# A second output layer as Strassen products in two sweeps, in a fused attention and two-layer gated network kernel

## The chip, the cores and the metric

The kernel runs on one core of one Trainium2 chip. The metric is the device time of one execution in microseconds. Before the change the median of three runs is 1741.35 us (1739.97 to 1743.14).

## What is computed

```
kv  = k^T v                      per batch (8) and head (8), 576 tokens, width 64
a   = q kv ;  a = a / rms(a) * g
x   = a as 4608 tokens x 512
x   = (sigmoid(x w_gate) * (x w_val)) w_out          512 -> 1536 -> 512
out = elu(x w_in) w_out2                             512 -> 2048 -> 512
```

All arrays are float32, and the weights arrive as 64-bit words that the kernel decodes.

## The kernel before, in words

**Tokens and groups.** The 4608 tokens are 12 blocks of 384. Two blocks make a group (`NG` = 6), and a hidden pair `fp` is two hidden chunks of 128. The kernel runs the first layer for all six groups (attention of group g+1 is mixed into the products of group g), then the second layer for all six. The second layer takes two stages a group: `in2` (eight pairs) and `out2`.

**Three matmuls for one.** Every float32 operand is split into a high and a low fp32r part. `matmul3` (L346 to L350) issues high x high, high x low, low x high into one accumulator, so each product of the text is three matmuls on lines L348, L349, L350.

**Strassen in the input layers.** `quad` computes a 2x2 block product (two hidden chunks by two token blocks) with seven products of six matmuls of 384 columns. `sides` (L450 to L466) prepares the token sides: differences on POOL and DVE (L458 to L463), then for each of seven sides a high part on ACT (L464) and a low part on DVE (L465). The sums over products are DVE additions that read PSUM (L485). Weight sums are made by `sums` on POOL when a weight is decoded, and come back with the stored high and low parts through `stream`.

**The plain output layer.** `out2` (L602 to L620) takes each hidden chunk and each token block, lets `split` (L546 to L552) make a J tile (high on ACT L550, low on DVE L552), and multiplies it by the chunk's 512 weights:

```python
for f in range(NF2):
    if f % 2 == 0:
        s, ld = stream("O", f // 2)
    for blk in in_blocks(f, NF2):
        j, dj = split(*hs[f // 2][f % 2, blk])
        for i in range(TPB):
            matmul3(acc[blk][i].slot, j.slot[:, 0, i*P:i*P+P], j.slot[:, 1, i*P:i*P+P],
                    v[:, f % 2, 0, :], v[:, f % 2, 1, :], f == 0, f == NF2 - 1)
```

A stage is 16 chunks x 2 blocks x 3 token chunks x 3 = 288 matmuls of 512 columns with the token chunk stationary, into six PSUM banks. Copies (L557, L558) and stores (L620) follow the last chunk.

**What sets the order.** `Plan` holds tasks with planned durations, buffer classes and due times, and writes out one fixed order for each engine and for SP, which issues every DMA. PE's order is the order in which the program adds products. Buffers that matter here: `S` (weights, 5 of 8 KB per partition), `J` (3 of 3 KB), `v` (54 blocks of 1.5 KB), `raw` (3), `wk` (4), `kv` (3), and eight PSUM banks in classes `psi` and `psa`. The first group runs plain products (`in1_plain`) while weights are decoded (`decode`, L260 to L303).

Of the kernel before, what the change touches and what calls it, by code (L numbers as in the profile page):

```python
# [9 lines left out]
F32 = mybir.dt.float32  # L10
# [11 lines left out]
P = 128  # L22
# [13 lines left out]
MMW = DM / 2400 + 0.0126  # L36
# [15 lines left out]
class Task:  # L52
    def __init__(self, eng, dur, fn, after, bufs, due, seq):
        self.eng, self.dur, self.fn, self.bufs, self.slack, self.seq = eng, dur, fn, bufs, due, seq
        self.after = {id(t): t for t in after if t is not None}.values()
        self.next, self.wait, self.ready, self.early, self.started = [], 0, 0.0, None, None


class Plan:
# [12 lines left out]
    def add(self, eng, dur, fn, after=(), bufs=(), due=None, queue=None):  # L72
# [6 lines left out]
        return t  # L79

# [36 lines left out]
    def round(self):  # L117
        self.set_due()
        for t in self.tasks:
            t.wait, t.ready = len(t.after), 0.0  # L120
            for b in t.bufs:
                b.left, b.slot = 0, None
# [28 lines left out]
        def begin(t, at):  # L151
# [7 lines left out]
            push(at + t.dur, "end", t)  # L159

# [45 lines left out]
def tile_kernel(ctx: ExitStack, tc: tile.TileContext, kv, kvtail, qt, g2, w1, w2, out):  # L206
# [49 lines left out]
    last_hi = [None]  # L256

    def decode(layer, fp, after=None):

        src, idx = (w1, "gvo".index(layer)) if layer in "gvo" else (w2, "IO".index(layer))  # L260
        order = (2 * fp, 2 * fp + 1) if layer in "oO" else (2 * fp + 1, 2 * fp)
        wh, wp = plan.buf("wk", "wh"), plan.buf("wk", "wp")
        word = []
        for n, f in enumerate(order):
# [14 lines left out]
        sa = plan.buf("S", "dec" if layer in "gvo" else "dec2")  # L279
        if layer in "oO":  # L280
            hi = lambda: sa.slot.rearrange("q b t n -> q (b t n)").rearrange("q (f t n) -> q f t n", f=2, t=2)
            x_hi, x_lo, src_w = (lambda: hi()[:, :, 0, :]), (lambda: hi()[:, :, 1, :]), lambda: wh.slot
        else:
            x_hi, x_lo = (lambda: sa.slot[:, :, 0, :]), (lambda: sa.slot[:, :, 1, :])
            src_w = lambda: wh.slot.rearrange("q f (k n) -> q (f k) n", k=2)
        h = add("ACT", 1.05, lambda: nc.scalar.activation(x_hi(), src_w(), AF.Copy), [w, last_hi[0]], [wh, sa])
        last_hi[0] = h
        l = add("DVE", 1.3, lambda: nc.vector.tensor_tensor(x_lo(), src_w(), x_hi().bitcast(F32), op=ALU.subtract), [h], [wh, sa])
        if layer in "oO":
            d = (wo1 if layer == "o" else wo2)[fp]  # L290
            written[layer, fp] = [dma(P * 8192, lambda: nc.sync.dma_start(
# [443 lines left out]
```

## Time and profile before

| | |
|---|---|
| median of 3 runs | 1741.35 us |
| the profiled execution | 1741.11 us, its span 1739.3 us, mean granted clock 0.991 |
| PE busy | 1704.1 us, 98% of the span, 9359 matmuls |
| DVE, ACT, POOL busy | 971.6, 757.1, 258.6 us |
| DMA | 431.57 MB, 68.4% of 16 engines' span on SP's queue |

The rest of the execution's time, 1.8 us, lies around the span. A busy PE means that matmul records cover the time; since matmuls are pipelined and their ends modelled, the pace is read from starts and counts, not from the duration of one.

### The profile page before, as it was taken

To read this page: it belongs to the slowest core of one execution; us is meant where nothing else is said; L and a number is where in the kernel's file an instruction comes from. 1 tells how busy PE (TensorE), PEld (TensorE's weight loads), DVE (VectorE), ACT (ScalarE), POOL (GpSimd) and SP (SyncE) were. 2 spreads that over 40 slices of the span, in tenths; PEclk is the share of its full clock that TensorE was granted. 3 is DMA by queue.
4 is the path that set the end of the run, shared out by engine and by line. 5 is a ranking of instruction groups with operands and counts; after the bars stand their busy time and mean duration, and the time that the engine had idled before them with its cause. 6 is when DMAs were issued, how large, how long until landed. Compare 5 with 4: busy or idle time off the path is not lost.

```text
span 1739.3 us, 25106 instructions
## 1 busy us (share of the span) xinstructions
PE 1704.1 (98%) x9359; PEld 1609.7 (93%) x9359; DVE 971.6 (56%) x1752; ACT 757.1 (44%) x1527; POOL 258.6 (15%) x244
## 2 busy tenths in 40 slices
PE   6899999999999999999899999999999999999998
PEld 5799999999999999999899998898998998998987
DVE  5466647854485376458444465465465455555542
ACT  4455433542263245226213364364353453443542
POOL 0001236411140132124122001001001001001000
PEclk8899999999999999999999999999999999999999
DMA  9597988798579768867867476475574673773751
GB/s 347 177 347 262 339 276 291 258 352 320 220 267 358 258 242 318 324 231 259 312 252 283 146 257 220 166 266 184 197 281 142 224 271 129 248 266 116 260 203 59
DMA packets 94443, 431.57 MB, mean 248 GB/s; under 512 B 10608, under 2 KB 29040, under 8 KB 66928
## 3 DMA queue, kind: packets, MB, share of 16 engines
q1 hardware_dynamic: 94320, 429.96, 68.4%
q8 instruction: 74, 1.21, 0.3%
q14 instruction: 49, 0.40, 0.1%
HBM read 353.37 MB, written 76.55 MB: 247 GB/s over the span
## 4 chain that ended last, share of the span: by engine, by line
PE 91%; DVE 4%; DMA 3%; ACT 1%; issue 1%; SPq 0%; DVEq 0%; ACTq 0%
PE psi L348 23%; PE psi L350 23%; PE psi L349 22%; PE psa L349 6%; PE psa L350 6%; PE psa L348 6%; PE psa L396 2%; PE psa L370 2%; DMA wsI<-S 2%; PE psa L435 1%; PE psa L372 1%; DVE J L552 1%; DMA kv<-kv 1%; DVE wk L272 1%; DMA S<-wsv 0%
## 5 line engine op out<-in xcount | busy, mean ns | idle before, releaser
L485 DVE TENSOR_TENSOR v<-v,psi 128x384 f32<-128x384 f32 x540 | 298.4, 553 | 336.2 <-PE psi L350 328.1
L348 PE MATMUL psi<-x,S 128*128 128x384 f32 x1056 | 361.8, 343 | 1.1 <-DMA S<-wsv 1.1
L349 PE MATMUL psi<-x,S 128*128 128x384 f32 x1056 | 355.0, 336 | 0.0
L350 PE MATMUL psi<-x,S 128*128 128x384 f32 x1056 | 354.9, 336 | 0.0
L552 DVE TENSOR_TENSOR J<-v,J 128x384 fp32r<-128x384 f32 x336 | 200.3, 600 | 257.1 <-ACT J L550 257.1
L550 ACT ACTIVATE J<-v 128x384 fp32r<-128x384 f32 x336 | 175.3, 523 | 326.2 <-PE psa L349 116.6
L348 PE MATMUL psi<-xt,S 128*128 128x384 f32 x648 | 220.6, 340 | 2.7 <-DMA S<-wsv 2.7
L350 PE MATMUL psi<-xt,S 128*128 128x384 f32 x648 | 217.3, 335 | 0.0
L349 PE MATMUL psi<-xt,S 128*128 128x384 f32 x648 | 217.0, 335 | 0.0
L348 PEld LDWEIGHTS psi<-x,S 128*128 128x128 f32 x1056 | 199.9, 189 | 4.5 <-DMA S<-wsv 1.4
L349 PEld LDWEIGHTS psi<-x,S 128*128 128x128 f32 x1056 | 199.8, 189 | 0.4 <-DVE x L443 0.2
L350 PEld LDWEIGHTS psi<-x,S 128*128 128x128 f32 x1056 | 199.5, 189 | 0.0
L521 POOL TENSOR_TENSOR v<-v,v 128x384 f32<-128x384 f32 x90 | 98.5, 1098 | 410.8 <-DVE v L485 366.1
L460 POOL TENSOR_TENSOR v<-v,v 128x384 f32<-128x384 f32 x22 | 24.9, 1130 | 773.8 <-DVE v L458 747.5
L348 PEld LDWEIGHTS psi<-xt,S 128*128 128x128 f32 x648 | 122.0, 188 | 3.8 <-issue 3.0
L596 ACT ACTIVATE v<-v 128x384 f32<-128x384 f32 x144 | 75.4, 524 | 108.8 <-DVE v L485 108.8
L349 PEld LDWEIGHTS psi<-xt,S 128*128 128x128 f32 x648 | 121.9, 188 | 0.0
L350 PEld LDWEIGHTS psi<-xt,S 128*128 128x128 f32 x648 | 121.9, 188 | 0.0
L489 ACT ACTIVATE v<-psi 128x384 f32<-128x384 f32 x108 | 53.1, 492 | 137.1 <-PE psi L350 130.9
L350 PE MATMUL psa<-S,J 128*128 128x512 f32 x288 | 112.7, 391 | 0.0
L350 PE MATMUL psi<-S,J 128*128 128x512 f32 x288 | 112.6, 391 | 0.0
L349 PE MATMUL psa<-S,J 128*128 128x512 f32 x288 | 112.2, 389 | 0.0
(96 smaller groups left out, 2979.8 us busy)
## 6 DMA issues: line engine op xcount, KB each, us to landing
S<-wsI SPq DMA_DIRECT2D x48, 1024.0 KB, 5.1
S<-wsO SPq DMA_DIRECT2D x48, 1024.0 KB, 5.0
S<-wso SPq DMA_DIRECT2D x36, 1024.0 KB, 6.2
S<-wsI SPq DMA_DIRECT2D x48, 768.0 KB, 5.9
raw<-w SPq DMA_DIRECT2D x68, 512.0 KB, 6.4
S<-wsg SPq DMA_DIRECT2D x24, 1024.0 KB, 5.8
S<-wsv SPq DMA_DIRECT2D x24, 1024.0 KB, 5.2
S<-wsg SPq DMA_DIRECT2D x30, 768.0 KB, 6.8
```

Of the source, the lines that this page charges most:

```text
L348: nc.tensor.matmul(acc, wh, xh, start=first, stop=False, skip_group_check=more)
L349: nc.tensor.matmul(acc, wh, xl, start=False, stop=False, skip_group_check=more)
L350: nc.tensor.matmul(acc, wl, xh, start=False, stop=last, skip_group_check=more)
L370: nc.tensor.matmul(o, k[:, 0, c, :], k[:, 1, c, :], start=(c == 0), stop=False)
L396: nc.tensor.matmul(v[lo - t0:hi - t0, i, :], qb.slot[:, lo - j * BLK:hi - j * BLK], kvb[b % 2][:, p, :], start=True, stop=True)
L460: k2 = add("POOL", T_POOL, lambda t=t2, a=b22, b=t1: nc.gpsimd.tensor_tensor(t.slot, a.slot, b.slot, op=ALU.subtract), [k1, d22], [t2, b22 ...
L485: return add("DVE", T_DVE, lambda: nc.vector.tensor_tensor(dst.slot, a.slot, bank[k].slot[:, :BLK], op=ALU.add), after, [dst, a, bank[k]])
L489: s1 = add("ACT", T_ACT, lambda: nc.scalar.activation(t1.slot, bank["a"].slot[:, :BLK], AF.Copy), [p1], [t1, bank["a"]])
L521: t = add("POOL", T_POOL, lambda r=r, b=b: nc.gpsimd.tensor_tensor(r.slot, r.slot, b.slot, op=ALU.mult), [d, s], [r, b])
L550: hi = add("ACT", T_ACT, lambda: nc.scalar.activation(j.slot[:, 0, :], f.slot, AF.Copy), [d], [j, f])
L552: lo = add("DVE", 0.5, lambda: nc.vector.tensor_tensor(j.slot[:, 1, :], f.slot, j.slot[:, 0, :].bitcast(F32), op=ALU.subtract), [hi], [j, f])
L596: a1 = add("ACT", T_ACT, lambda e=e, b=b: nc.scalar.activation(e.slot, ps_or_v(b), AF.Relu, scale=-1.0), [d], [e, b])
```

## The change

It touches five things.

1. **Second output layer** (`out_stage`, `Tokens`, `out2`). Each stage becomes seven products for each of eight hidden pairs, 9 matmuls of 256 columns each (3 token chunks x 3), token chunk stationary, half of the outputs moving. Four accumulators a, b, c, d take two PSUM banks each, all eight. In sweep 1, pair by pair, a and c then b and d are summed; `middle` copies a and adds up outputs from b, c and d; in sweep 2 a, c and d take three further products for each pair; `end` forms three outputs.
2. **Token sides of the output layer.** The sides are made in place on POOL in the hidden buffers: one subtraction in `in2` (L586), three in `out_stage` (L650, L651, L656) for each pair. `split` now takes two blocks at a time (128x768).
3. **Two-block buffers.** Features and hidden values sit in `hp` (21 of [P, 2, 384]); `sides` works on 128x768; `v` shrinks to 11, `J` becomes 4 of 6 KB.
4. **Weights in 4 KB pieces.** `S` becomes 7 of 4 KB. A pair of an input layer is loaded as four DMAs (512, 512, 512, 256 KB) where it was two; a pair of the second output layer as 512, 512, 512 and 256 KB where it was one of 1024 KB.
5. **Decode in place.** High and low parts are written over the raw words; the decodes of second-layer weights move from four after each of groups 1 to 4 to six, six and four after groups 1 to 3. The units of the first group run in another order, and the first key/value loads use the three `kv` buffers alone.

The core of the diff:

```diff
-    slots("v", 54, [P, BLK], F32)
-    slots("S", 5, [P, 4, 2, 256], F32R)
-    slots("J", 3, [P, 2, BLK], F32R)
+    slots("hp", 21, [P, 2, BLK], F32)
+    slots("v", 11, [P, BLK], F32)
+    slots("S", 7, [P, 2, 2, 256], F32R)
+    slots("J", 4, [P, 2, 2, BLK], F32R)
...
+    def stream(layer, fp):
+        d, res = (ws2 if layer == "I" else ws1["gv".index(layer)])[fp], {}
+        for names, view in ((("A11", "S2"), d[:, 0:5:4]), (("S1", "S3"), d[:, 3:6:2]), (("A12", "S4"), d[:, 1:7:5]), (("A22",), d[:, 2:3])):
+            t, ld = load(view, written[layer, fp])
+            res.update({n: (t, i, ld) for i, n in enumerate(names)})
+        return res
...
-            t, view, ld = load_kv(b, p, "wk" if first and p > 1 else "kv")
+            t, view, ld = load_kv(b, p, "kv")
...
+    def t1_in_place(hp, t):
+        k = add("POOL", T_POOL, lambda: nc.gpsimd.tensor_tensor(
+            hp[0].slot[:, 1, :], hp[0].slot[:, 1, :], hp[0].slot[:, 0, :], op=ALU.subtract), [t["11"], t["12"]], [hp[0]])
+        return hp, [t["11"], k], [t["21"], t["22"]]
...
+    def out_stage(layer, hs, parts, mm_of, finish):
+        nf = len(hs)
+        acc = {k: [plan.buf("psa" if k in "ac" else "psi") for _ in parts] for k in "abcd"}
...
+        def first_half(fp):
+            hp, d1, _ = hs[fp]
+            s, ld = stream_out(layer, fp, 0, 0)
+            j, jv, dj = split(lambda: hp[0].slot, 2, d1, hp[0], "JA")
+            last["a"] = product("a", 0, j, jv, 0, s, ld + dj, fp == 0)
+            last["c"] = product("c", 1, j, jv, 1, s, ld + dj, fp == 0)
+            return dj
+        def second_half(fp, dj):
+            hp, d1, d2 = hs[fp]
+            s, ld = stream_out(layer, fp, 0, 1)
+            H = lambda k, e: hp[k].slot[:, e, :]
+            k2 = add("POOL", T_POOL, lambda: nc.gpsimd.tensor_tensor(H(0, 1), H(1, 1), H(0, 1), op=ALU.subtract), dj + d2, hp)
+            k3 = add("POOL", T_POOL, lambda: nc.gpsimd.tensor_tensor(H(0, 0), H(0, 1), H(0, 0), op=ALU.subtract), [k2], [hp[0]])
+            j, jv, dj2 = split(lambda: hp[0].slot, 2, [k3], hp[0], "JB")
+            last["b"] = product("b", 0, j, jv, 1, s, ld + dj2, fp == 0)
+            last["d"] = product("d", 1, j, jv, 0, s, ld + dj2, fp == 0)
+            return add("POOL", T_POOL, lambda: nc.gpsimd.tensor_tensor(H(0, 1), H(1, 0), H(0, 1), op=ALU.subtract), dj2 + d2, hp)
+        k4, dj = {}, {}
+        for fp in range(nf + 1):
+            if fp < nf:
+                dj[fp] = first_half(fp)
+            if fp:
+                k4[fp - 1] = second_half(fp - 1, dj[fp - 1])
+        got = finish.middle(acc, last)
+        done = {}
+        for fp in range(nf):
+            hp, _, d2 = hs[fp]
+            s, ld = stream_out(layer, fp, 1, 0)
+            j, jv, dj_ = split(lambda hp=hp: hp[1].slot, 2, d2 + [k4[fp]], hp[1], "JA")
+            done["a"] = product("a", 1, j, jv, 0, s, ld + dj_, False, got["a"])
+            s4, ld4 = stream_out(layer, fp, 1, 1)
+            done["c"] = product("c", 0, j, jv, 1, s4, ld4 + dj_, False, got["c"])
+            j, jv, dj_ = split(lambda hp=hp: hp[0].slot[:, 1:2, :], 1, [k4[fp]], hp[0], "JB")
+            done["d"] = product("d", 0, j, jv, 0, s, ld + dj_, False, got["d"])
+        finish.end(acc, done)
...
+    W2 = (0, 6, 6, 4, 0, 0)
```

PE, at the start of the output stage of the first group of the second layer. `psa` are accumulators, S the weights, J the token chunks. Before:

```order
L348 MATMUL psa_155<-S_134,J_135 128x512
L349 MATMUL psa_155<-S_134,J_135 128x512
L350 MATMUL psa_155<-S_134,J_135 128x512
L348 MATMUL psa_156<-S_134,J_135 128x512
L349 MATMUL psa_156<-S_134,J_135 128x512
```

Now:

```order
L420 MATMUL psa_136<-S_113,J_115 128x256
L421 MATMUL psa_136<-S_113,J_115 128x256
L419 MATMUL psa_137<-S_113,J_115 128x256
L420 MATMUL psa_137<-S_113,J_115 128x256
L421 MATMUL psa_137<-S_113,J_115 128x256
```

A matmul now moves 256 columns; a bank takes two token chunks and the next bank the third. Over the program 1728 matmuls of 512 columns are gone and 3024 of 256 are there; the 6840 of 384 columns stay.

POOL, in sweep 1 of the same stage, from the third pair on (`hp` are hidden buffers, written in place); before, POOL had only the sides of the next group there (L459, L460, L463):

```order
L650 TENSOR_TENSOR hp_90<-hp_93,hp_90 128x384
L651 TENSOR_TENSOR hp_90<-hp_90 128x384
L650 TENSOR_TENSOR hp_91<-hp_84,hp_91 128x384
L651 TENSOR_TENSOR hp_91<-hp_91 128x384
L656 TENSOR_TENSOR hp_90<-hp_93,hp_90 128x384
L650 TENSOR_TENSOR hp_86<-hp_92,hp_86 128x384
L651 TENSOR_TENSOR hp_86<-hp_86 128x384
L656 TENSOR_TENSOR hp_91<-hp_84,hp_91 128x384
```

Three subtractions for each pair are new work on POOL; those of the first two pairs stand ahead of this place, among the last pairs of `in2`. From here to the last pair's L651 there are 16.

DVE, at the end of sweep 1 and the start of sweep 2 (L686 is the low part of a J, L536 that of a side of the next group, L754 an addition out of an accumulator):

```order
L536 TENSOR_TENSOR x_72<-hp_82,x_72 128x2x384
L686 TENSOR_TENSOR J_115<-hp_95,J_115 128x2x384
L686 TENSOR_TENSOR J_118<-hp_88,J_118 128x2x384
L536 TENSOR_TENSOR xt_73<-hp_78,xt_73 128x2x384
L686 TENSOR_TENSOR J_116<-hp_77,J_116 128x2x384
L536 TENSOR_TENSOR x_71<-hp_94,x_71 128x2x384
L754 TENSOR_TENSOR wk_122<-wk_123,psi_134 128x512
L754 TENSOR_TENSOR wk_122<-wk_123,psi_132 128x256
L754 TENSOR_TENSOR wk_123<-wk_122,psa_138 128x512
L754 TENSOR_TENSOR wk_123<-wk_122,psa_139 128x256
L754 TENSOR_TENSOR wk_123<-wk_123,psi_133 128x512
L754 TENSOR_TENSOR wk_123<-wk_123,psi_135 128x256
```

The third row is the last J of sweep 1. From the first J of the third pair to it DVE has 12 J halves and 5 other instructions with two inputs in SBUF. The six additions run without a split between them, and the next row after them is the first J of one block in sweep 2.

## Rows read from the trace of the kernel before

**Rows 1.** The page: busy time of the engines, and the granted TensorE clock in 40 slices (tenths).
```profile
PE 1704.1 (98%) x9359; PEld 1609.7 (93%) x9359; DVE 971.6 (56%) x1752; ACT 757.1 (44%) x1527; POOL 258.6 (15%) x244
...
PEclk8899999999999999999999999999999999999999
```

**Rows 2.** Busy time by stretch: start:end, length, then each engine's busy time with its instructions, the granted clock, the DMA engines' share and GB/s. First key/value products, rest of the first group's plain products, rest of the first layer, second layer.
```profile
0.00:30.00 30.00, 16.36 (x84) 12.75 (x84) 13.60 (x32) 14.37 (x29) 1.63 (x8) 0.84 0.89 334
30.00:174.00 144.00, 134.76 (x775) 128.50 (x774) 90.15 (x156) 77.90 (x145) 5.32 (x4) 0.94 0.75 273
174.00:991.00 817.00, 809.16 (x4759) 795.10 (x4758) 481.61 (x849) 319.14 (x634) 214.96 (x203) 1.00 0.77 280
991.00:1739.00 748.00, 743.87 (x3748) 673.32 (x3746) 386.24 (x718) 345.73 (x721) 36.71 (x30) 1.00 0.58 205
```

**Rows 3.** The same view for one output stage and the input stage after it, and for 60 us inside an output stage.
```profile
1049.60:1115.30 65.70, 65.70 (x290) 53.94 (x289) 30.44 (x52) 24.18 (x49) 7.34 (x6) 1.00 0.48 170
1115.30:1173.60 58.30, 58.30 (x338) 58.28 (x337) 35.74 (x72) 34.13 (x74) 0.00 (x0) 1.00 0.72 260
...
1300.00:1360.00 60.00, 60.00 (x265) 49.24 (x264) 27.73 (x46) 21.21 (x44) 7.34 (x6) 1.00 0.45 163
```

**Rows 4.** PE in order of time at the stages' seams: start, duration (both us), instruction.
```profile
1049.63 0.39 PE L348 MATMUL psa<-S,J 128*128 128x512 f32 x1
...
1115.09 0.39 PE L350 MATMUL psa<-S,J 128*128 128x512 f32 x1
1115.31 0.33 PE L348 MATMUL psi<-x,S 128*128 128x384 f32 x1
...
1173.58 0.39 PE L348 MATMUL psa<-S,J 128*128 128x512 f32 x1
```

**Rows 5.** Groups by line and shape: count, busy us, mean ns of one, idle before. One of the six groups of 512-column matmuls, the float32 matmuls of 128 columns, and three groups of weight loads (PEld).
```profile
L348 PE MATMUL psa<-S,J 128*128 128x512 f32 x288 | 112.1, 389 | 0.0
...
L396 PE MATMUL psa<-kvb,v 128*128 128x128 f32 x256 | 41.9, 292 | 0.0
...
L348 PEld LDWEIGHTS psi<-x,S 128*128 128x128 f32 x1056 | 199.9, 189 | 4.5 <-DMA S<-wsv 1.4 <-DVE v L485 0.9
...
L348 PEld LDWEIGHTS psa<-S,J 128*128 128x128 f32 x288 | 54.1, 188 | 10.9
...
L396 PEld LDWEIGHTS psa<-kvb,v 128*128 128x128 f32 x256 | 37.0, 198 | 3.7 <-issue 3.6
```

**Rows 6.** PE and its weight loads in order of time: six matmuls of 128 columns in a row, merged (start, whole length).
```profile
398.41 0.83 PE L396 MATMUL psa<-kvb,v 128*128 128x128 f32 x6
...
398.24 0.81 PEld L396 LDWEIGHTS psa<-kvb,v 128*128 128x128 f32 x6
```

**Rows 7.** Groups by line and shape on DVE, ACT and POOL.
```profile
L485 DVE TENSOR_TENSOR v<-v,psi 128x384 f32<-128x384 f32 x540 | 298.4, 553 | 336.2 <-PE psi L350 328.1 <-ACT J L550 5.7 <-ACT v L597 1.1
L552 DVE TENSOR_TENSOR J<-v,J 128x384 fp32r<-128x384 f32 x336 | 200.3, 600 | 257.1 <-ACT J L550 257.1
...
L318 DVE TENSOR_TENSOR S<-wk,S 128x1024 fp32r<-128x1024 f32 x20 | 25.9, 1294 | 11.5 <-ACT S L315 11.5
...
L557 DVE COPY kv<-psi 128x512 f32<-128x512 f32 x6 | 4.2, 692 | 15.1 <-PE psi L350 15.1
...
L550 ACT ACTIVATE J<-v 128x384 fp32r<-128x384 f32 x336 | 175.3, 523 | 326.2 <-PE psa L349 116.6 <-PE psi L349 101.7 <-PE psa L350 51.2
...
L521 POOL TENSOR_TENSOR v<-v,v 128x384 f32<-128x384 f32 x90 | 98.5, 1098 | 410.8 <-DVE v L485 366.1
```

**Rows 8.** POOL and DVE in order of time where both work on SBUF (the sides of a group, made beside an output stage).
```profile
1573.68 1.21 POOL L460 TENSOR_TENSOR v<-v,v 128x384 f32<-128x384 f32 x1 [1.02 <-ACT x L464]
1574.86 2.62 POOL L459 TENSOR_TENSOR v<-v,v 128x384 f32<-128x384 f32 x2
...
1576.52 1.37 DVE L552 TENSOR_TENSOR J<-v,J 128x384 fp32r<-128x384 f32 x1
...
1582.27 0.55 DVE L552 TENSOR_TENSOR J<-v,J 128x384 fp32r<-128x384 f32 x1
1582.74 0.55 DVE L465 TENSOR_TENSOR xt<-v,xt 128x384 fp32r<-128x384 f32 x1
1583.21 0.55 DVE L465 TENSOR_TENSOR x<-v,x 128x384 fp32r<-128x384 f32 x1
```

**Rows 9.** POOL's multiplications of L521: shortest, median and longest in ns.
```profile
L521 POOL TENSOR_TENSOR v<-v,v x90: 994/1016/1920, 241.9 to 941.5; 128x384 f32<-128x384 f32 x90
```

**Rows 10.** DMA issues: count, KB each, median us from issue to landing.
```profile
S<-wsO SPq DMA_DIRECT2D x48, 1024.0 KB, 5.0
S<-wso SPq DMA_DIRECT2D x36, 1024.0 KB, 6.2
...
kv<-kv SPq DMA_DIRECT2D x30, 512.0 KB, 7.7
```

**Rows 11.** PE where it waited in the first layer (in brackets the idle time and its releaser).
```profile
48.44 0.80 PE L370 MATMUL psa<-kv 128*128 128x128 f32 x2 [5.14 <-DMA kv<-kv]
...
70.22 0.98 PE L435 MATMUL psa<-ident,v 128*128 128x128 f32 x6 [1.86 <-DVE v L427]
...
855.86 0.44 PE L348 MATMUL psi<-x,S 128*128 128x384 f32 x1 [1.06 <-DMA S<-wsv]
```

More of the change, by code (lines that the diff above doesn't have):

```diff
@@ L79, in add, with follow @@
         return t
+    def follow(self, chain, t):
+        if chain:
+            t.behind = chain[-1]
+            chain[-1].followed.append(t)
+        chain.append(t)
     def set_due(self):
@@ L119, in round @@
         for t in self.tasks:
-            t.wait, t.ready = len(t.after), 0.0
+            t.wait, t.ready = len(t.after) + (t.behind is not None), 0.0
             for b in t.bufs:
@@ L159, in begin @@
             push(at + t.dur, "end", t)
+            for d in t.followed:
+                d.wait -= 1
+                if not d.wait:
+                    push(max(at, d.ready), "ready", d)
         for t in self.tasks:
@@ L286, in decode @@
[L286 to L291, printed above, removed]
-                out=d.rearrange("q f t n -> q (f t n)"), in_=sa.slot.rearrange("q b t n -> q (b t n)").bitcast(F32)), [h, l], [sa])]
-            return sa, [h, l]
@@ new lines, in load @@
+    def load(view, after, early=15.0):
+        t = plan.buf("S")
+        ld = dma(P * 4096, lambda: nc.sync.dma_start(out=t.slot[:, :view.shape[1]].bitcast(F32), in_=view), after, [t], early=early)
+        plan.follow(chain, ld)
+        return t, [ld]
+    def stream(layer, fp):
[3 more added lines that the diff above has]
+            res.update({n: (t, i, ld) for i, n in enumerate(names)})
+        return res
@@ new lines, in fresh @@
+        sums = add_up(wh, ld, sf)
+        t, la = load(d[:, 0:2], written[layer, fp])
+        res["A11"], res["A12"] = (t, 0, la), (t, 1, la)
+        for i in (0, 2):
+            x = plan.buf("S")
+            src = lambda i=i: quarters(sf)[:, i:i + 2, :]
+            h = add("ACT", 0.6, lambda x=x, src=src: nc.scalar.activation(x.slot[:, :, 0, :], src(), AF.Copy), sums, [sf, x])
+            h.early = 12.0
+            plan.follow(chain, h)
+            l = add("DVE", 0.75, lambda x=x, src=src: nc.vector.tensor_tensor(
+                x.slot[:, :, 1, :], src(), x.slot[:, :, 0, :].bitcast(F32), op=ALU.subtract), [h], [sf, x])
+            written[layer, fp] = written[layer, fp] + [dma(P * 4096, lambda x=x, i=i: nc.sync.dma_start(out=d[:, 3 + i:5 + i], in_=x.slot.bitcast(F32)), [h, l], [x])]
+            res[f"S{i + 1}"], res[f"S{i + 2}"] = (x, 0, [h, l]), (x, 1, [h, l])
@@ L467, in sides, with product @@
         return X, done
     def quad(layer, fp, X, done, weights=stream):
-        (sa, sb_), (ld_a, ld_b) = weights(layer, fp)
+        W = weights(layer, fp)
         bank = {k: plan.buf("psi") for k in "abcd"}
-        def product(k, half, i, x, first, last, after=()):
-            s, ld = (sa, ld_a) if half == "A" else (sb_, ld_b)
+        def product(k, name, x, first, last, after=()):
+            s, i, ld = W[name]
             def mm():
@@ L565, in out1, with split @@
+    x2_there = {}
+    def split(view, n, after, b, kind):
+        j = plan.buf("J", kind)
+        jv = lambda t: j.slot[:, :n, t, :]
+        hi = add("ACT", 0.24 + 0.32 * n, lambda: nc.scalar.activation(jv(0), view(), AF.Copy), after, [j, b])
+        hi.early = 14.0
+        lo = add("DVE", 0.25 + 0.4 * n, lambda: nc.vector.tensor_tensor(jv(1), view(), jv(0).bitcast(F32), op=ALU.subtract), [hi], [j, b])
+        return j, jv, [hi, lo]
     def out1(g, hs):
-        acc = {blk: [plan.buf("psi" if blk == 0 else "psa") for _ in range(NCC)] for blk in range(2)}
+        acc = {blk: [plan.buf("psi" if blk else "psa") for _ in range(NCC)] for blk in range(2)}
@@ L623, in tile_kernel, with mm @@
+    def out2(g, hs):
+        def mm(bank, q, ws, xs, first):
+            lo, hi = Tokens.COLS[q]
+            for i in range(lo, hi):
+                o, r = bank.slot[:, (i - lo) * 256:(i - lo) * 256 + 256], slice(i * P, i * P + P)
+                matmul3(o, xs[0][:, r], xs[1][:, r], ws[0], ws[1], first and i == lo, True, not (first and i == lo))
+        out_stage("O", hs, [6 * MMH, 3 * MMH], mm, Tokens(g))
     nc.vector.memset(gcol, 0.0)
```

449 lines of the change are left out of this document (256 added, 193 removed).

## The prediction, on record before the change was timed

> **What bounds the kernel now.** I read the busy times first: PE is covered for 98% of the span at the full granted clock, DVE for 56%, ACT for 44%, POOL for 15% [rows 1]. Then the stretches: the second layer is 748 us with 4 us of PE idle, the first layer after its first group 817 us with 8 us, and only the first 174 us lose more (23 us idle and a clock of 0.84 and 0.94) [rows 2]. So time falls if PE has fewer columns to stream, and only where the next engine keeps up. The stage that the change rewrites is seen in the seams: an output stage runs from 1049.63 to 1115.31, 65.68 us for 288 matmuls, and the input stage behind it to 1173.58, 58.27 us for 336 [rows 4]. PE does not wait in either, while DVE works 30 of 66 us and POOL 7 [rows 3].
>
> **The pace of a matmul of 256 columns.** 384 columns cost 58.27 / 336 = 173.4 ns [rows 4]; 512 cost 60 / 265 = 226.4 ns [rows 3]. That is 0.414 ns a column, so 128 columns fewer than 384 give 173.4 - 53 = 120 ns. The trace has no matmul of 256 columns, so I bound it. From above: not more than the 173.4 ns of 384 columns, which carries the same weight load. From below: six float32 matmuls of 128 columns, each with a load, take 0.83 us [rows 6]; less the 0.29 us that the last one is recorded with [rows 5], they start 0.54 / 5 = 108 ns apart. A load's record is 188 to 198 ns whatever the matmul [rows 5], yet pairs follow at 108 and 173, so the record is latency, and loads do not hold PE at 120. I take 120, on the line through two shapes of the same data type.
>
> **Part 1, the output stage.** 1728 matmuls of 512 columns go, 3024 of 256 come: 504 a stage. 504 x 0.120 = 60.5 us, against 65.7: 5.2 us less, 31 us over six stages. This is the gain; what follows takes from it.
>
> **Part 2, the sides on POOL and DVE in sweep 1.** A pair takes PE four products of nine matmuls, 4.32 us. Beside it POOL makes three subtractions and DVE two low parts of 768 columns. The trace shows that such instructions exclude each other: DVE's low part that starts at 1576.52 takes 1.37 us instead of 0.55 and ends 0.41 us after POOL's second instruction of that run does, at 1577.48 [rows 8]. From the same rows: POOL and one DVE instruction of 384 take 2.62 / 2 = 1.31 us; DVE alone starts one every 0.47 us; so POOL holds the SBUF access for about 0.84 us of its 0.99 [rows 8, 9]. A DVE low part of 768 columns holds it longer by 384 x 1.16 ns (1294 ns for 1024 columns against 0.55 us for 384 [rows 7, 8]): about 0.9 us. A pair alone needs 3 x 0.84 + 2 x 0.9 = 4.3 us of it in 4.32. By the order, from the third pair to the last low part of sweep 1 it is 16 POOL instructions and 17 of DVE, 13.4 + 15.3 = 28.7 us, in the 15 half steps (2.16 us each, 32.4 us) before PE needs that part. The first two pairs' sides are made in the input stage, and two buffers of each J kind give about 4 us of slack. It fits, at 89%, with little left when an instruction comes late: between 0 and 4 us a stage are lost; I take 1.0. It is nearest to the row for the access alone, since no chain there is longer than the slack.
>
> The Trainium skill ("SBUF — State Buffer", "Who interferes with whom") has a rule against this place: a VectorE instruction with two SBUF inputs and a GpSimd one that reads SBUF lock each other out for the whole instruction. The trace agrees on the lock and gives a shorter hold, 0.84 of 0.99 us and 0.47 of 0.55 [rows 8, 9]. Whole instructions would make 16 x 0.99 + 17 x 1.0 = 32.8 us for the 32.4, a sweep without slack, and the sum 10 us or more higher; without a lock it would be 6 us lower. I go by the measured holds.
>
> **Part 3, between the sweeps.** Sweep 2 adds into c and d, so DVE must first have read b, c and d. The order has six additions in a row and then a low part of 384 columns. By rows, 0.69 us for 512 columns and 0.69 - 128 x 1.08 ns x 2 = 0.41 for 256 [rows 7]: 3 x 1.10 + 0.47 = 3.8 us from about 0.2 us before b ends. PE has d of sweep 1 and a and c of sweep 2 in between, 3.24 us. It waits 0.6 us for d (0.3 to 1.0; not a gain). From the end of a stage to the next input stage b's banks are free, and 2 us of products run on them while DVE clears d: no wait.
>
> **Part 4, weights.** A pair of the output layer loads 1.75 MB instead of 1 MB. A stage moves 170 GB/s x 65.7 us = 11.2 MB now [rows 3], 17.5 MB then, 280 GB/s at about 0.8 of the DMA engines. The first layer runs at 280 GB/s and 0.77 for 817 us [rows 2] with few waits such as the 1.06 us at 855.86 [rows 11]. With seven buffers a load in sweep 2 goes out 7.6 us or more ahead of its use; such loads land in 5.0 to 6.2 us [rows 10]. Cost nothing; the cover gone, a load late by 1 us costs that each time. The input stages load the same bytes in four pieces, with 10 us of lead. SP issues 478 DMAs more, each behind the release of a buffer that PE needs no sooner.
>
> **Part 5, the first layer.** The same 384-column matmuls, so no gain by count. The first group can move either way. Against it: the fourth key/value load waits for a buffer; a load lands in 7.7 us [rows 10], some 2 us later than now. For it: the 5.14 us at 48.44 and 1.86 us at 70.22 [rows 11], with the lower clock around them, are up for a new order. Later, six decodes where four ran add some 8 MB to groups 1 and 2, 50 GB/s on 280 [rows 2]: 0.9 of the DMA engines. Unknown: -6 to +12 us, taken as 0. Its price is nearest to the row of the 817 us, which shows that this stretch absorbs transfers.
>
> **The sum.** 504 x 0.120 + 1.0 + 0.6 + 0.2 (the seam that the 65.68 hold) = 62.3 us a stage, 3.4 less. Six stages: 20 us. The profiled execution took 1741.11 us (1739.3 us of span and 1.8 around it), so 1721; it stands 0.2 us below the median of the runs, and I leave the number at **1721 us**.
>
> **Rivals.**
> 1. *No wait shows and the first group gains.* For it: the 28.7 us do fit, and 7 us of waits in the first 71 us are there to be lost [rows 11]. 1741 - 31 - 4 = 1706.
> 2. *The SBUF access becomes the bound of sweep 1 (slower).* Each hand-over between POOL and DVE adds to 4.3 us a pair; if what one pair is late is passed to the next, a sweep stretches. It decides at 4.6 us a stage with Part 3's 0.6, or 0.6 us a pair. With 1.2 us a pair (access taken in turn by 5.8 instructions with 0.2 us between) over eight pairs it is 9.6 us less the 2 us that the early pairs give: 1741 + 6 x (7.6 + 0.6 - 5.2) = 1759. For it: 4.3 of 4.32. Against it: head start and slack, 89% by the order.
> 3. *The first layer pays.* DMA at 0.9 of its time and decodes in place make weights late: +15 us on 1721, 1736, about no change. For it: the wait at 855.86 and the first slices' load. Against it: 0.77 with 8 us of idle in 817.
> 4. *Weight loads set the pace at 256 columns (slower).* Halfway between 120 and 173, 147 ns: 74.1 us a stage, 1741 + 6 x (74.1 + 1.6 - 65.7) = 1801. It decides at 127 ns with the waits of Parts 2 and 3. For it: no row has 256 columns, and the counts of the order leave no doubt that they will be there. Against it: 108 ns at 128 columns, with a load each.
>
> **How the numbers follow.** My case 0.52 (1713 to 1732), rival 1 0.17 (1703 to 1713), rival 2 0.14, rival 3 0.12 (half of it faster, half within 0.2%), rival 4 0.05. Two tenths of a per cent, 3.5 us, is what a measurement of this kernel can tell from no change. Faster: 0.52 + 0.17 + 0.06 = 0.75; the same 0.06; slower 0.14 + 0.05 = 0.19. The range takes the first case with rivals 1 and 3 and the near end of rival 2: 1703 to 1746. My case and rival 1 alone, 1703 to 1732, hold 0.69.
>
> **What would show it.** Right: matmuls of 256 columns 120 ns apart; an output stage of 61 to 63 us; input stages at 58.3; waits of PE below 1 us at the seam of the sweeps, put down to L754 or L686; POOL's L650 and L651 and DVE's L686 with mean times a third above their shortest. Wrong: a pace above 127 ns; PE waiting for L686 or L651 at every pair of sweep 1; PE waiting for loads of `wsO` in sweep 2; the first 991 us of the span moved by more than 8 us.

## The result and the profile after

The changed kernel takes 1765.22 us (median of 4 runs, 1763.76 to 1770.66) where the kernel before takes 1742.24 on the same chip: a ratio of 1.0136, 95% interval 1.0109 to 1.0164. It is slower, by 23 us; the forecast was 1721 and faster. The profiled execution has a span of 1761.9 us.

The page of the changed kernel: busy times, as [rows 1], and PE's busy tenths in 40 slices.

```profile
PE 1691.4 (96%) x10655; PEld 1662.5 (94%) x10655; DVE 1125.7 (64%) x1694; ACT 786.4 (45%) x1432; POOL 538.4 (31%) x435
...
PE   5999999999999999999999998998998998998998
```

PE has 13 us less to do and is covered for 96% instead of 98%: the time went into waits. POOL's time has doubled. The slices with an 8 stand one in three in the second layer: the loss returns once in each group.

The stretches, as [rows 2, 3]: the second layer, the first output stage, the input stage after it, and the last output stage.

```profile
994.70:1757.50 762.80, 731.49 (x5042) 725.44 (x5040) 528.23 (x724) 381.23 (x685) 290.23 (x207) 0.98 0.78 251
1053.60:1123.00 69.40, 62.57 (x505) 62.16 (x504) 50.41 (x49) 29.56 (x43) 35.08 (x22) 0.95 0.72 234
1123.00:1181.90 58.90, 58.88 (x339) 58.25 (x338) 40.24 (x74) 34.56 (x73) 14.87 (x13) 1.00 0.85 277
1696.80:1757.40 60.60, 60.60 (x505) 60.44 (x504) 34.87 (x41) 24.67 (x36) 25.52 (x19) 1.00 0.66 210
```

The two output stages to compare are the second and the fourth row. Both stream the same 504 matmuls of 256 columns. The last one, which has no next group behind it, is 60.6 us of PE without a gap at the full clock; the other is 69.4 us with 6.8 us of PE idle and a clock of 0.95. The loss is in the stage that also makes the sides of the next group: DVE 50 us instead of 35, POOL 35 instead of 26.

PE at the seams, as [rows 4]: first output stage, first matmul after it, last output stage.

```profile
1053.58 0.28 PE L419 MATMUL psa<-S,J 128*128 128x256 f32 x1
...
1122.97 0.28 PE L421 MATMUL psi<-S,J 128*128 128x256 f32 x1
1123.10 0.34 PE L419 MATMUL psi<-x,S 128*128 128x384 f32 x1
...
1696.82 0.28 PE L419 MATMUL psa<-S,J 128*128 128x256 f32 x1
...
1757.16 0.28 PE L421 MATMUL psi<-S,J 128*128 128x256 f32 x1
```

From the first matmul to the last, the five output stages with sides take 69.39, 69.99, 70.34, 69.02 and 69.78 us, and the last 60.34 for 503 steps, 120.0 ns a matmul. The balance against the trace of before:

| stretch | before, us | after, us | difference |
|---|---|---|---|
| up to the second layer's first matmul | 991.39 | 994.75 | +3.4 |
| six input stages, each | 58.07 to 58.09 | 58.63 to 58.65 | +3.3 in all |
| five output stages with sides, each | 65.45 to 65.46 | 69.02 to 70.34 | +21.2 in all |
| last output stage | 65.09 | 60.34 | -4.8 |
| seams between stages | | | -0.5 in all |
| last matmul | 1734.48 | 1757.16 | +22.7 |

What PE waited for in the first output stage (engine, line, releaser: total us, times, longest).

```profile
ACT J L684 <- PE psa L420: 18.5, 12, 3.6
...
PE psa L419 <- DVE wk L754: 5.0, 1, 5.0
...
PE psi L421 <- DVE J L686: 1.9, 1, 1.9
```

PE has two waits: 1.9 us for the last low part (L686) of sweep 1, and 5.0 us for the additions between the sweeps (L754). The first row is ACT's wait for PE before the high parts. What DVE and POOL did ahead of them, in order of time (start, duration, instruction, in brackets idle time and its releaser; the fence has DVE):

```profile
1058.85 1.81 DVE L686 TENSOR_TENSOR J<-hp,J 128x768 fp32r<-128x768 f32 x1 [1.19 <-ACT J L684]
...
1074.59 1.77 DVE L686 TENSOR_TENSOR J<-hp,J 128x768 fp32r<-128x768 f32 x1
1076.28 1.77 DVE L529 TENSOR_TENSOR hp<-hp,hp 128x768 f32<-128x768 f32 x1
1077.98 1.78 DVE L686 TENSOR_TENSOR J<-hp,J 128x768 fp32r<-128x768 f32 x1
1079.68 0.95 DVE L536 TENSOR_TENSOR x<-hp,x 128x768 fp32r<-128x768 f32 x1
...
1083.93 4.26 DVE L686 TENSOR_TENSOR J<-hp,J 128x768 fp32r<-128x768 f32 x2
1088.28 2.44 DVE L536 TENSOR_TENSOR xt<-hp,xt 128x768 fp32r<-128x768 f32 x1
1090.64 1.77 DVE L686 TENSOR_TENSOR J<-hp,J 128x768 fp32r<-128x768 f32 x1
1092.33 2.55 DVE L536 TENSOR_TENSOR x<-hp,x 128x768 fp32r<-128x768 f32 x1
1094.80 1.00 DVE L754 TENSOR_TENSOR wk<-wk,psi 128x512 f32<-128x512 f32 x2
```

and POOL:

```profile
1075.62 1.61 POOL L651 TENSOR_TENSOR hp<-hp 128x384 f32<-128x384 f32 x1
1077.20 1.73 POOL L656 TENSOR_TENSOR hp<-hp,hp 128x384 f32<-128x384 f32 x1
...
1081.58 1.61 POOL L651 TENSOR_TENSOR hp<-hp 128x384 f32<-128x384 f32 x1
1083.15 1.72 POOL L656 TENSOR_TENSOR hp<-hp,hp 128x384 f32<-128x384 f32 x1
1084.84 2.53 POOL L530 TENSOR_TENSOR hp<-hp,hp 128x768 f32<-128x768 f32 x1
1087.33 2.56 POOL L531 TENSOR_TENSOR hp<-hp,hp 128x768 f32<-128x768 f32 x1
1089.86 1.72 POOL L656 TENSOR_TENSOR hp<-hp,hp 128x384 f32<-128x384 f32 x1
1091.55 2.51 POOL L534 TENSOR_TENSOR hp<-hp,hp 128x768 f32<-128x768 f32 x1
```

A DVE low part of 768 columns takes 0.95 us (1079.68, POOL waiting behind it); beside a half step of POOL (here: one of its subtractions of 384 columns, L650, L651, L656) its record is 1.77, beside one of the three long subtractions of the sides (L530, L531, L534) about 2.5. The two engines take turns: DVE starts at 1074.59, 1076.28 and 1077.98, one POOL instruction between each, a period of 1.70 us. DVE instructions of this size that nothing disturbs start 0.87 us apart, so a half step of POOL holds the access for 0.83 us and a long one for about 1.6 (2.53 less 0.95). From 1072.1 to 1094.8 there are 12 such instructions of DVE and 8 short and 3 long ones of POOL: 10.4 + 6.6 + 4.8 = 21.8 of 22.7 us. The access was full, and the additions, which DVE's order has behind all of this, started at 1094.80, 41.2 us into the stage. In the last stage they start 33.5 us in:

```profile
1730.31 1.01 DVE L754 TENSOR_TENSOR wk<-wk,psi 128x512 f32<-128x512 f32 x2
```

From 1093.5 us, still inside the 5 us wait, the clock is at its lower level, 1.2 GHz, for 6.8 us:

```profile
1093.50:1100.30 6.80, 3.84 (x18) 3.84 (x19) 5.95 (x10) 1.68 (x2) 0.56 (x1) 0.50 0.07 12
```

Matmuls start 0.21 us apart there instead of 0.12, 18 of them, some 1.7 us more. With the 7 us of waits that is the 9.1 us by which this stage exceeds the last one.

### The profile page after: what moved, and what is told of

It reads as the page before. It is cut to its first block, busy times and chain, and to the rows that moved or that the text cites. A ratio compares the mean times of both kernels' runs of the same rounds, so it can differ in the third digit from the quotient of the medians.

```text
span 1761.9 us, 28817 instructions
## 1 busy us (share of the span) xinstructions
PE 1691.4 (96%) x10655; PEld 1662.5 (94%) x10655; DVE 1125.7 (64%) x1694; ACT 786.4 (45%) x1432; POOL 538.4 (31%) x435
## 4 chain that ended last, share of the span: by engine, by line
PE 88%; DVE 5%; issue 2%; DMA 2%; POOL 2%; ACT 1%; DVEq 0%; SPq 0%; ACTq 0%
PE psi L419 22%; PE psi L421 21%; PE psi L420 21%; PE psa L419 6%; PE psa L420 6%; PE psa L421 6%; PE psa L467 2%; PE psa L441 2%; DVE J L686 1%; DMA kv<-kv 1%; DVE x L536 1%; PE psa L507 1%; PE psa L443 1%; POOL hp L530 1%; DVE hp L529 1%
## 5 line engine op out<-in xcount | busy, mean ns | idle before, releaser
L686 DVE TENSOR_TENSOR J<-hp,J 128x768 fp32r<-128x768 f32 (+1 forms) x264 | 293.8, 1128 | 134.2 <-ACT J L684 133.8
L684 ACT ACTIVATE J<-hp 128x768 fp32r<-128x768 f32 (+1 forms) x264 | 206.5, 784 | 225.7 <-PE psa L420 112.6
L419 PE MATMUL psa<-S,J 128*128 128x256 f32 x576 | 167.3, 291 | 21.8 <-DVE wk L754 21.8
L601 POOL TENSOR_TENSOR hp<-hp,v 128x384 f32<-128x384 f32 x90 | 104.8, 1170 | 262.1 <-DVE v L556 206.1
L586 POOL TENSOR_TENSOR hp<-hp 128x384 f32<-128x384 f32 x48 | 52.1, 1086 | 401.3 <-DVE hp L727 401.3
L420 PE MATMUL psa<-S,J 128*128 128x256 f32 x576 | 166.3, 289 | 0.0
L421 PE MATMUL psa<-S,J 128*128 128x256 f32 x576 | 166.1, 288 | 0.0
L419 PEld LDWEIGHTS psa<-S,J 128*128 128x128 f32 x576 | 114.3, 198 | 22.8 <-DVE wk L754 22.8
L421 PE MATMUL psi<-S,J 128*128 128x256 f32 x432 | 125.3, 290 | 9.4 <-DVE J L686 9.4
L419 PEld LDWEIGHTS psi<-xt,S 128*128 128x128 f32 x648 | 121.7, 188 | 6.4 <-DVE v L556 5.6
L420 PE MATMUL psi<-S,J 128*128 128x256 f32 x432 | 124.9, 289 | 0.0
L419 PE MATMUL psi<-S,J 128*128 128x256 f32 x432 | 124.9, 289 | 0.0
```

The lines of the kernel that those rows point to most:

```text
L419: nc.tensor.matmul(acc, wh, xh, start=first, stop=False, skip_group_check=more)
L420: nc.tensor.matmul(acc, wh, xl, start=False, stop=False, skip_group_check=more)
L421: nc.tensor.matmul(acc, wl, xh, start=False, stop=last, skip_group_check=more)
L586: k = add("POOL", T_POOL, lambda: nc.gpsimd.tensor_tensor(hp[0].slot[:, 1, :], hp[0].slot[:, 1, :], hp[0].slot[:, 0, :], op=ALU.subtract), ...
L601: t[n] = add("POOL", T_POOL, lambda r=r, b=b: nc.gpsimd.tensor_tensor(r(), r(), b.slot, op=ALU.mult), [d, s[n]], [e, b])
L684: hi = add("ACT", 0.24 + 0.32 * n, lambda: nc.scalar.activation(jv(0), view(), AF.Copy), after, [j, b])
```

## The experiments

Three readings of the loss stood against each other at first, and a fourth, D, came after the first four of these kernels. A: POOL's three long instructions lock DVE out. B: it is DVE's fixed order, six instructions of the sides ahead of the additions, whoever holds the access. C: POOL's half steps against DVE's low parts, as the prediction's second rival had it. D: the sum of all that needs the access before the additions, sides included. Every kernel starts from the changed one; line numbers shift by one to five where lines were added. Edits to the second layer also move the planner's order in the first layer (its second layer begins between 987.6 and 1004.1 us), so stages are compared, not totals alone; which edit moves the first layer by how much is open but for one kernel below.

**The sides' subtractions on DVE** (in both layers; k3 and the subtraction for xt4 as k2 here).

```diff
-        k2 = add("POOL", 2.2, lambda: nc.gpsimd.tensor_tensor(t2.slot, b22.slot, t1.slot, op=ALU.subtract), [k1] + d22, [t2, b22, t1])
+        k2 = add("DVE", 1.0, lambda: nc.vector.tensor_tensor(t2.slot, b22.slot, t1.slot, op=ALU.subtract), [k1] + d22, [t2, b22, t1])
```

> The changed kernel with the three subtractions of the next group's sides (768 wide, 2.5 us each on POOL beside DVE) on DVE; POOL keeps the half steps of sweep 1. Theory A (the sides' long POOL instructions keep DVE from the SBUF in the last third of sweep 1, and the additions of the seam come late): the 2.0 us wait for J and the 3.6 to 5.1 us wait for the additions fall under 1.5 us together, an output stage from 69.7 to 62 us, about 1728 us in all. Theory B (the order alone: DVE has the sides' instructions in front of the additions, whoever holds the SBUF): DVE has eight of them in front now where it had six, so 69 to 71 us a stage, 1762 to 1770. Theory C (POOL's half steps against DVE's low parts, rival 2 of the prediction): the waits stay at 6 us or more a stage, 1755 to 1765.

Measured: 1742.47 us, ratio to the kernel before 1.0002 (0.9989 to 1.0015). An output stage takes 64.97 us, and 1.3, 0.6 and 1.7 us of waits stay in the first. Neither A's 62 nor B's 69 to 71, and the 3.6 us of waits are not C's 6 or more. The two rows ahead of the seam show what is left:

```profile
1094.28 0.95 DVE L534 TENSOR_TENSOR hp<-hp,hp 128x768 f32<-128x768 f32 x1
1095.14 1.01 DVE L754 TENSOR_TENSOR wk<-wk,psi 128x512 f32<-128x512 f32 x2
```

The additions start 38.1 us into the stage, 3.1 earlier than in the changed kernel: three holds of 1.6 on POOL became three of 0.87 on DVE, but all of them still stand ahead (that is 2.2 of the 3.1 us; the rest, 0.87, is one low part of the sides that the planner moved behind the additions). None of the three readings fits alone; a sum of them is left.

**The sides held back into sweep 2.**

```diff
-    def sides(xa, xb):
+    def sides(xa, xb, early=None):
+
+        def add(*a, **k):
+            t = plan.add(*a, **k)
+            t.early = early
+            return t
...
-        X, done = sides(load_x2(g, 0), load_x2(g, 1))
+        X, done = sides(load_x2(g, 0), load_x2(g, 1), 22.0)
```

> The changed kernel with the next group's sides held back until 22 us before they are due, which puts them behind the additions of the seam, into sweep 2. Theories A and B: the stage of each group is that of the last group, which has no sides, 60.4 to 61.5 us, and the input stages keep 58.7; 1765 - 5 x 8.7 = 1721 us, up to 1728 if a side comes late for the input stage. Theory C: sweep 1 keeps its waits, 66 to 69 us a stage, 1747 to 1762.

Measured: 1741.00 us, ratio 1.0000 (0.9986 to 1.0013); stages of 63.99 us. In sweep 1 and at the seam no wait is left, with all half steps still on POOL: C falls as a cause by itself. A and B put the stage at 60.4 to 61.5 us and the total at 1721 to 1728, and missed that too. One wait came up in sweep 2, where the sides now are; PE, and DVE beside POOL's last long subtraction (which starts at 1108.00):

```profile
PE psa L421 <- DVE J L691: 1.9, 1, 1.9
```

```profile
1108.31 2.60 DVE L541 TENSOR_TENSOR x<-hp,x 128x768 fp32r<-128x768 f32 x1
...
1111.70 1.41 DVE L691 TENSOR_TENSOR J<-hp,J 128x768 fp32r<-128x768 f32 x2
```

The second layer is 28.7 us shorter than in the changed kernel (733.7 instead of 762.4 from first to last matmul); the total hides 9.3 of it, since the first layer came out longer by that.

**The half steps on DVE**, the sides' long subtractions on POOL (k3 and the third half step, L656, as k2 here).

```diff
-            k2 = add("POOL", T_POOL, lambda: nc.gpsimd.tensor_tensor(H(0, 1), H(1, 1), H(0, 1), op=ALU.subtract), dj + d2, hp)
+            k2 = add("DVE", T_DVE, lambda: nc.vector.tensor_tensor(H(0, 1), H(1, 1), H(0, 1), op=ALU.subtract), dj + d2, hp)
```

> The changed kernel with the half steps of sweep 1 (three subtractions a pair, 384 wide) on DVE; POOL has the sides' three long ones alone. DVE has 2 x 0.95 + 3 x 0.55 = 3.6 us a pair in 4.3 us of PE. Theory C: no lock in the half steps any more, 60.5 to 62 us a stage, 1720 to 1730. Theory A: DVE still meets three instructions of POOL that hold the access for up to 2.5 us, and has less room: 64 to 68 us a stage, 1735 to 1757. Theory B: DVE's order is longer by 1.6 us a pair, 70 us or more, 1765 or more.

Measured: 1728.12 us, ratio 0.9918 (0.9902 to 0.9935); stages of 62.13 us, less than A's range and far from B's. C came nearest, with its total in range and the stage 0.1 us above it, but C alone could not explain the kernel before this one. Three small waits are left:

```profile
PE psi L421 <- DVE J L686: 0.5, 2, 0.4
PE psa L419 <- DVE wk L754: 0.5, 1, 0.5
```

With 73 instructions on DVE, 24 more, the stage is 7.6 us shorter than the mean of the changed kernel's. DVE holds the access for 0.47 us where POOL's half step holds it for 0.83. That is not the whole of it: the planner also put less of the sides ahead of the additions, three instructions on DVE instead of six and two long ones on POOL instead of three, so the 7.6 us are not the price of the half steps alone. The input stages went from 58.64 to 58.07 us, which is the value of before: the first two pairs' half steps cost 0.57 us there.

**Two of the first key/value loads in the weights' buffers, as before.**

```diff
...
-            t, view, ld = load_kv(b, p, "kv")
+            t, view, ld = load_kv(b, p, "wk" if first and p > 1 else "kv")
```

(The line left out adapts the view of such a buffer.)

> The changed kernel with one thing undone: two of the first four key/value loads go into buffers of the weights' class again, as before the change, so that none waits for a buffer. The output stages are as in the changed kernel under every theory (69.7 us). If the first layer's 3.4 us more come from the start (first plain product at 38.2 us instead of 29.9): 3 to 8 us less, 1757 to 1762. If the start is won back later whatever it is, as the first layer of the changed kernel suggests (8.3 us late at 38 us, 3.4 us late at 991): 0 to 3 us less, 1762 to 1765.

Measured: 1759.44 us, ratio 1.0095 (1.0078 to 1.0111), and stages as in the changed kernel (68.98 to 70.27 us). The first plain product, in the changed kernel and in this one:

```profile
38.24 0.67 PE L419 MATMUL psi<-x,S 128*128 128x384 f32 x1
```

```profile
29.64 0.67 PE L419 MATMUL psi<-x,S 128*128 128x384 f32 x1
```

8.6 us at the start, of which 7.1 are left when the second layer begins (987.63). In this pair the first layer's +3.4 us comes from the shared buffers; without that it is 3.8 us shorter than before. It is not the only thing that moves this layer: the kernel with the half steps on DVE, with the buffers shared, starts its plain products at 30.5 us and its second layer at 1000.7.

**The low parts of the sides held back, their subtractions not.**

```diff
+            done[n][1].early = early
...
-        X, done = sides(load_x2(g, 0), load_x2(g, 1))
+        X, done = sides(load_x2(g, 0), load_x2(g, 1), 22.0)
```

> The changed kernel with the low parts of the next group's sides alone held back until 22 us before they are due (they fall into sweep 2); the sides' first DVE subtraction and POOL's long ones stay in sweep 1. If the lock by POOL's long instructions is the whole loss (theory A): 4 us or more of waits stay at the end of sweep 1, 66 us or more a stage, 1748 or more. If DVE's queue in front of the additions is the whole loss (theory B): none stay, 60.4 us a stage but for sweep 2. If it is the sum of all that needs the access in sweep 1, sides included (theory D: 28.7 us of half steps and low parts, 0.9 for each sides' instruction of DVE, about 1.7 for each long one of POOL, against 32.4 us and 4 us of slack): 28.7 + 0.9 + 3.4 = 33 us fit, no wait above 0.7 us in sweep 1; in sweep 2 the held back low parts meet POOL, and about 2 us stay there as in the kernel with all sides late. B and D: 62 to 64 us a stage, 1728 to 1745.

Measured: 1726.20 us, ratio 0.9907 (0.9876 to 0.9938); stages of 61.95 us, just below what B and D had. Two of POOL's three long instructions stand about as late as before, 29.9 and 32.5 us into the stage (31.3 and 33.8 in the changed kernel); the third needs a low part that is held back and falls into sweep 2. The loss is 1.6 us instead of 9.4, and the wait at the end of sweep 1 is 0.9 us where A had 4 or more: A falls. This wait is at the end of sweep 1 (D had at most 0.7 there), and none came in sweep 2 where I expected it. What waited from 1084 to 1093:

```profile
DVE J L687 <- ACT J L685: 5.1, 2, 3.4
ACT xt L535 <- POOL hp L531: 2.0, 1, 2.0
...
PE psa L419 <- DVE wk L755: 0.9, 1, 0.9
```

POOL's result was late, the side's high part on ACT waited for it with the high part of the hidden values behind it, and DVE idled: ACT's order now, not DVE's.

**All of it on DVE, the sides spread from 30 us ahead, key/value loads as before**, and the same with one of the two kinds of POOL instructions put back (edits as above).

> The changed kernel with the half steps and the sides' subtractions all on DVE (POOL has nothing left in the output stages), the sides held back until 30 us before they are due, and the two key/value loads in the weights' buffers. Theory D: no lock at all, DVE needs 17 x 0.95 + 24 x 0.47 + 4 x 0.95 = 31 us in sweep 1 and some 26 in the 27.6 us of sweep 2: 60.4 to 61 us a stage and 58.1 in the input stages. With the first layer at 987 to 996 us: 1706 to 1717. Theory B (DVE's queue): with 45 instructions of DVE before the additions the stage is 64 us or more, 1728 or more.

Measured: 1708.43 us, ratio 0.9803 (0.9778 to 0.9827). All six output stages are 60.35 us, all input stages 58.07; the first output stage and the input stage before it:

```profile
1045.80:1106.20 60.40, 60.40 (x505) 60.40 (x505) 50.16 (x76) 30.53 (x45) 1.27 (x1) 1.00 0.83 272
987.50:1045.70 58.20, 58.20 (x338) 58.20 (x337) 38.66 (x74) 35.28 (x73) 7.13 (x7) 1.00 0.83 268
```

DVE is as busy as in the changed kernel (50.2 and 50.4 us) with 76 instructions instead of 49, since their records no longer contain waits for POOL, and PE has no gap in 60.4 us. B falls: from the stage's start to the additions DVE has 43 instructions with two inputs in SBUF, where the changed kernel has 23 (three of them for the sides, where it has six), and the additions start on time. This kernel is faster than the kernel before and the changed one; the 5.1 us a stage that Part 1 of the prediction put as the gain are there in full (65.45 to 60.35).

> As the kernel before this one, with the sides' three long subtractions on POOL. Theory D: DVE 17 x 0.95 + 24 x 0.47 + 3 x 0.95 = 30 us and one long instruction of POOL, 1.7, before the additions, 32 us of 32.4 and slack: at most 0.7 us of waits at the end of sweep 1, and up to 1 us in sweep 2, where two long ones of POOL meet 18 instructions of DVE; 60.5 to 62 us a stage, 1708 to 1722. Theory A: as long as POOL's long instructions run beside DVE's, 1.8 us a stage stay as with the half steps on DVE alone, 62.1 us.

Measured: 1729.26 us, ratio 0.9924 (0.9902 to 0.9946); stages of 64.17 to 64.47 us. All readings missed. The window ahead of the additions, DVE and then POOL:

```profile
1076.28 2.48 DVE L691 TENSOR_TENSOR J<-hp,J 128x768 fp32r<-128x768 f32 x1 [0.32 <-ACT J L689]
1078.80 2.10 DVE L661 TENSOR_TENSOR hp<-hp,hp 128x384 f32<-128x384 f32 x1
...
1083.42 1.00 DVE L759 TENSOR_TENSOR wk<-wk,psi 128x512 f32<-128x512 f32 x2
```

```profile
1076.09 1.86 POOL L535 TENSOR_TENSOR hp<-hp,hp 128x768 f32<-128x768 f32 x1 [25.50 <-DVE hp L534]
1077.89 2.59 POOL L536 TENSOR_TENSOR hp<-hp,hp 128x768 f32<-128x768 f32 x1
```

D's sum over a whole sweep was the wrong sum. Two long subtractions (the forecast had one) fit into the sweep, but they came 28.9 and 30.7 us into the stage, with DVE full from 1076.28 on: each adds about 1.55 us to a DVE record there, and the additions start 36.2 us in instead of 33.3. The kernel with the half steps on DVE has the same number of instructions of each kind ahead of its additions, with the two long ones 25.5 and 29.3 us into a stage that starts at 1058.90, and its stage is 2.0 us shorter:

```profile
1084.37 2.50 POOL L531 TENSOR_TENSOR hp<-hp,hp 128x768 f32<-128x768 f32 x1 [22.08 <-DVE hp L529]
1088.24 2.10 POOL L530 TENSOR_TENSOR hp<-hp,hp 128x768 f32<-128x768 f32 x1 [1.37 <-DVE J L686]
```

> As the kernel before this one, but the half steps on POOL and the sides' subtractions on DVE, held back until 30 us before they are due. Theory D: 28.7 us of half steps and low parts and 4 x 0.9 of sides before the additions, 32.3 us of 32.4 and 4 of slack: up to 1 us of waits, 60.5 to 62 us a stage, 1708 to 1722. Theory C (half steps of POOL against DVE): the waits of the kernel with the sides on DVE stay, 64 us or more, 1728 or more.

Measured: 1718.88 us, ratio 0.9867 (0.9844 to 0.9889); stages of 61.80 us with 0.8 and 0.2 us of waits, in D's range; C, which had 64 or more, misses.

Together they give one line. From the traces, for the first output stage: when the additions start after its first matmul, and its length.

| kernel | additions start, us | stage, us | difference, us |
|---|---|---|---|
| all on DVE, spread | 33.31 | 60.35 | 27.0 |
| changed kernel, last stage | 33.49 | 60.34 | 26.9 |
| half steps on POOL, sides on DVE, spread | 34.92 | 61.79 | 26.9 |
| low parts held back | 35.07 | 61.94 | 26.9 |
| half steps on DVE | 35.25 | 62.13 | 26.9 |
| half steps on DVE, sides spread on POOL | 36.23 | 64.17 | 27.9 |
| sides on DVE | 38.09 | 64.97 | 26.9 |
| changed kernel | 41.22 | 69.39 | 28.2 |

The stage is the start of the additions plus 26.9 us, and 1.0 and 1.3 us more where the lower clock follows. The additions can start when b of the last pair is summed, 279 matmuls of 120 ns or 33.5 us in: from there on every us by which DVE is late is a us of the stage. The line tells where the time is lost, not what makes DVE late; that is told by the kernels that differ in one edit. Against the one with all on DVE and the sides spread, the half steps on POOL cost 1.4 to 1.5 us a stage and the long subtractions on POOL 3.8 to 4.1. Holding the sides back is no gain by itself: it took 3.2 us off a stage with the half steps on POOL (64.97 to 61.80) and added 2.0 to 2.3 with the long subtractions there (62.13 to 64.17 and more); both pairs differ in the key/value loads as well, which alone left the stages as they were. Holding back all sides is the one kernel outside the line (33.50 and 63.99), with its wait in sweep 2.

## Why the prediction was wrong

**Pace (right).** 120.0 ns a matmul of 256 columns, 60.34 us a stage without waits against 60.5 predicted. Rival 4 is out.

**Part 2 (wrong, the step that failed).** The holds were right: 0.84 + 0.9 us for a half step and a low part predicted, a period of 1.70 measured. With the Trainium skill's rule, whole-instruction exclusion between POOL and DVE instructions with two SBUF inputs ("SBUF — State Buffer", "Who interferes with whom"), the trace agrees on the lock; whole records would give 1.02 + 0.95 = 1.97 us for the period, and 1.70 was measured. What failed was the list, and the stretch it was summed over. The list stopped at the POOL instruction that the last low part needs and counted 16. POOL does not stop there: as the engines take turns, its next two instructions, a half step (1083.15) and a long one of the sides (1084.84), 0.83 + 1.6 = 2.4 us, had the access before DVE's last low part of sweep 1 was through. Three more (1087.33, 1089.86, 1091.55), 4.0 us, had it before the additions. With the 2.4 us the sum over the sweep would still have fitted, 31.1 of 32.4 us. So the larger error is the sum over the whole sweep: up to 1071.8 DVE idles for 5.5 us, waiting for ACT's high parts, and from 1072.1 on the access is full. ACT in turn waits for PE (18.5 us in this stage); whether more J buffers would let both run ahead was not tried. Predicted loss 1.0 us, measured 1.9 for the low part alone.

**Part 3 (wrong in its start).** The additions were put 0.2 us before b ends. They began 5.6 us after it (b ends at 1089.2), behind three more low parts, two of the sides and one of sweep 2 (1088.28, 1090.64, 1092.33), each with a POOL instruction in front of it, the last with POOL's third long subtraction. Given their start, the part was too dear: six additions take 2.8 us (0.93 a pair, not 1.10), and where they start on time, as in the last stage, PE waits for none of them. I had put 0.6 us, though the terms beside it, 3.8 - 0.2 - 3.24, give 0.4. PE's wait was before c (`psa` in the row), not before d. The wait of 5.0 us, and the lower clock behind it, are not an error of the additions but of what stood ahead of them.

**The sum.** 62.3 us a stage was forecast, 60.34 is what the matmuls need, 69.7 is the mean with sides. The five losses of 9.4 us, 47 us in all, turn the -30 of the matmuls into +16.5; the first layer's 3.4, the input stages' 3.3 and the seams' -0.5 make it 22.7.

**Part 4 (right).** No wait of PE for a load of `wsO` or `wsI` in the second layer.

**Part 5 (its price missed, inside its bounds).** +3.4 us on 0. The buffer wait that I named as 2 us cost 8.6 at 38 us; the rest was won back, 5.4 us of it in the first layer's output stages (49.75 us each, 49.75 to 51.38 before). Missed altogether: 0.55 us in each input stage, from the early pairs' half steps, which the prediction placed there and put at nothing. Rival 3, which had this layer pay 15 us, did not come, and rival 1, which had no waits, did not either.

**Rival 2** had the right resource and sign at a chance of 0.14. Its point, 1759 us, was 7.6 us lost in sweep 1 and 0.6 between the sweeps, in all six stages; it came out at 9.4 us in five of six. That the numbers are close is luck, since its cause was another: a turn of both engines takes 1.70 us, no more than the two holds of the prediction (1.74) and without 0.2 us more at each hand-over, and pair by pair sweep 1 keeps up (the last stage and the kernel with all sides late show it). The second job in the same stretch decided.

## What to carry to other kernels

When two engines share an access, list everything that either of them issues up to the instruction that PE waits for, other jobs' instructions and those that overtake included, and sum the holds over the last stretch before that point, not over the whole stage. In a fixed order the price can be read, here in all kernels but one, in one number: how late the first instruction of the needed chain starts. An instruction moved to the idle engine is not free if it holds what the busy one needs: here POOL's 0.83 us stood for 0.47 on DVE, and with all of it on the busier engine, the sides spread, the second layer went from 762.4 to 712.2 us.

## What the runs showed of the hardware

A record of DVE contains its wait for the access: 0.95, 1.77 or 2.5 us for the same low part, so 64% busy was partly waiting. An addition with one input in PSUM is not held up; beside POOL's half step at 1043.04 (1.73 us) it keeps its 0.54 us, as the Trainium skill's section named above has it for instructions with one SBUF input:

```profile
1043.04 1.73 POOL L651 TENSOR_TENSOR hp<-hp 128x384 f32<-128x384 f32 x1
...
1043.82 0.54 DVE L556 TENSOR_TENSOR v<-v,psi 128x384 f32<-128x384 f32 x1
```

The granted clock fell to its lower level behind PE's waits of 5.0 us in the changed kernel (for 6.8 us), of 1.9 us in each of the five stages of the kernel with all sides late, and of 2.1 us in those of the kernel with the half steps on DVE and the sides spread on POOL (for 3.4 us each); it did not behind waits of 0.8 to 1.0 us. The length of the wait alone does not decide: the changed kernel's 1.9 us wait for the last low part is followed by full clock in its first, second and fifth output stage and by 3.4 us of the lower one in the third and fourth, and the kernel with the sides' subtractions on DVE has 3.4 us of it in the same two stages behind waits of 1.2 and 0.5 us. The stretch behind the 1.9 us wait of the changed kernel in the first and in the third stage:

```profile
1088.20:1091.30 3.10, 3.06 (x25) 3.06 (x25) 3.02 (x2) 3.08 (x6) 3.10 (x2) 1.00 0.02 5
1346.10:1349.50 3.40, 3.40 (x19) 3.40 (x18) 3.40 (x2) 2.54 (x5) 3.40 (x3) 0.50 0.00 0
```
